# Gate and up pieces of a gated MLP as two lists of equal length

## The chip, the cores and the metric

The kernel runs on one core of a Trainium2 chip. A core has a matrix engine (TensorE, PE in the profile; its weight loads are PEld), VectorE (DVE), ScalarE (ACT), GpSimd (POOL) and SyncE (SP), which issues the DMAs here. Matmul results go to PSUM, which has eight banks of 128 x 512 float32; everything else stands in SBUF. The metric is the device time of one execution in microseconds (us).

## The reference

```python
x = A_x                                     # 1 x 2048 x 576, bf16
xn = _layernorm(x, axis=-1)
qkv = (xn @ wqkv).reshape(B, S, 3, 32, 18)  # 32 heads of 18
...                                         # causal, window of 256, softmax
s = (softmax(q k^T * 18 ** -0.5) @ v).reshape(B, S, 576) @ wo
...
gate = xn @ w_gate                          # 576 x 4608
up = xn @ w_up                              # 576 x 4608
g = silu((sigmoid(gate) * up) @ w_down)     # 4608 x 576
return x + s * g
```

## The kernel before

**Chunks.** The 2048 tokens are worked in four chunks of 512. For each chunk: layer norm, the QKV projection, attention, the output projection (`build_wo`, line 734), gate and up (`build_ffn`, line 777), and the down projection with the final product (`f2`, lines 851 and 881, and `final_cols`). Program order is not execution order: every operation goes into a list with an engine, an estimated duration, a priority and what it depends on, and a planner (`schedule`) places them one after the other in simulated time, lowest estimated start plus priority x 40 ns first. Each engine's order is then fixed, and `emit` writes it out with semaphore waits. SyncE's queue of DMAs is one such order.

**Gate and up.** The hidden width of 4608 is cut into 36 tiles of 128 (`ft`). For one tile, gate and up are each nine matmuls of 64 contraction rows by 512 tokens, since 576 is 9 x 64. The array is used as two halves of 64 rows: gate always in rows 0 to 63, up always in rows 64 to 127, and `xn` and the weights are stored for both halves, in the orders of blocks `LO` and `UP`. A step is one gate piece and one up piece side by side. Gate runs `SKEW` = 3 pieces ahead of up:

```python
def f_a(e, ft=ft):
    for i in range(NA):
        if ft < NFT:
            r = step(e, 0, ft, i)
        if ft > 0:
            r = step(e, 1, ft - 1, NC - NA + i)
    return r
```

so each tile is three TensorE operations of three steps (`fa`, `fb0`, `fb1`). At the start of a chunk's gate/up work three gate pieces have no partner, and at its end three up pieces. Each tile's gate and up take one PSUM bank each, from banks 4 to 7. When gate is complete, ScalarE takes its tanh (line 763); then VectorE forms (tanh + 1) x up into `hT` (line 767), which frees the tile's banks. Weights come in 12 groups of three tiles, four DMAs a group, into a ring of three slots (`wgs`).

**Around it.** Score units of attention (line 589) use banks 0 to 3, all four at once; ScalarE takes their exponentials (line 607), and the value products (line 658) follow for a pair of head groups. The planner puts these units between gate/up operations. In chunk 0, SyncE's queue issues x, the QKV weights, weight groups 0, 1 and 2, then eight transposing DMAs of q and k (line 209), then weight group 3. The output projection's four blocks are copied by ScalarE (line 749) into `sat`, a ring of four slots, one slot a block; `final_cols` reads the slot in the product of line 916.

**The end.** The last output block is done in two column parts, 448 and 128. Each goes through tanh (line 912), two products (914, 916), an addition to x (918) and a store. The load of x for that block is given a slack of 5000 ns in the planner. After its last DMA, SyncE waits for the final value of every DMA semaphore, in order of their numbers, and the program ends:

```python
if e == "SP":
    for ln, v in enumerate(lane_cnt):
        if v > 0:
            eng.wait_ge(lanes[ln], v)
    eng.nop()
```

Of the kernel before, what the change touches and what calls it, by code (L numbers as in the profile page):

```python
# [12 lines left out]
P = 128  # L13
CH = 512
# [6 lines left out]
FG = 3  # L21
# [27 lines left out]
SKEW = 3  # L49
# [6 lines left out]
FB_CUTS = (0,3,6)  # L56
LAST = 448
W_GATE = 2
F2B = ((0, 1), (2, 3), (6, 7), (4, 5))
# [110 lines left out]
class Builder:  # L170
# [97 lines left out]
    def build(self):  # L268
# [22 lines left out]
        for c in range(NCH):  # L291
# [6 lines left out]
            self.build_attn(c)  # L298
            self.op_pkz = [self.op("POOL", 2000, lambda e: e.memset(self.pk[:, 1:RPK, :, :], 0.0), f"pkz:{c}",
# [420 lines left out]
    def build_wo(self, c):  # L720
        self.op_wop = [None] * QPC
        self.op_s = [None] * QPC
        for pair in ((0, 2), (1, 3)):
# [22 lines left out]
            for qi, ps, (ss, _) in zip(pair, ps2, slots):  # L746
# [4 lines left out]
                self.op_s[qi] = (ss, se)  # L751
                self.op_wop[qi] = wo

    def build_ffn(self, c):
        mms = []
        pg, pu, slots, dmas = [], [], [], []
        wrel = {}

        def th_mul(ft, o_g, o_u):
            st_, dt_ = self.r_t.take()  # L760

            def f_th(e, st_=st_, ps=pg[ft]):
                return e.activation(self.tring[:, st_, :], self.bank(ps), ACTF.Tanh, scale=0.5)  # L763
            th = self.rd("ACT", act_ns(CH), f_th, f"th:{c}:{ft}", deps=[o_g] + dt_, prio=1, psum=[pg[ft]])

            def f_mul(e, st_=st_, ft=ft, ps=pu[ft]):
                return e.scalar_tensor_tensor(self.hT[:, ft, :], self.tring[:, st_, :], 1.0, self.bank(ps),  # L767
                                              ALU.add, ALU.mult)
            war = [self.f2_last[ft // WDG]] if self.f2_last else []
            mul = self.rd("DVE", dve_ns(CH), f_mul, f"hm:{c}:{ft}", deps=[th, o_u] + war, prio=1, psum=[pu[ft]])  # L770
# [3 lines left out]
        def step(e, gu, ft, i):  # L774
            r0 = 64 * gu
            fl = ft % FG
            return e.matmul(self.bank((pg, pu)[gu][ft]), self.wgs[r0:r0 + 64, slots[ft // FG], i, fl * P:(fl + 1) * P],  # L777
                            self.xn[r0:r0 + 64, i, :], start=(i == 0), stop=(i == NC - 1), tile_position=(r0, 0))
        NA = SKEW
        for ft in range(NFT + 1):  # L780
            if ft < NFT:
                if ft % FG == 0:
                    fg = ft // FG
                    sw, dw = self.r_w.take()
                    slots.append(sw)
                    wp = W_PRIO[fg] if c == 0 and fg < RW else -2
                    fc = slice(fg * FG * P, (fg + 1) * FG * P)
                    ws = self.load9(self.wgs[0:64, sw, :, :], self.wgs[64:P, sw, :, :], self.wg[:, fc],
                                    self.wu[:, fc], f"w:{c}:{fg}", ("w", sw),
                                    dw + ([self.w_gate] if c > 0 and fg < RW else []), wp,  # L790
                                    W0_FACTOR if c == 0 and fg < 5 else 1.42)
                    dmas.append(ws)
                    if c == 0 and fg in QKT_BEHIND:
                        for o in self.op_qkt[QKT_BEHIND[fg]:]:
                            o.behind = ws[-1:]
                pg.append(Psum((6,), (7,), (5,), (4,)))
                pu.append(Psum((6,), (7,), (5,), (4,)))
            war = [self.f2_last[ft // WDG]] if self.f2_last and ft < NFT else []
# [361 lines left out]
```

## Time and profile before

| | |
|---|---|
| three runs, median (range) | 570.92 us (570.83 to 571.53) |
| the profiled execution | 571.24 us |
| its span, first to last instruction | 569.0 us |
| TensorE busy | 560.6 us (99%) |
| VectorE, ScalarE busy | 304.8 us (54%), 274.7 us (48%) |
| gate and up matmuls, line 777 | 2592, busy 298.8 us |
| down projection matmuls, lines 851 and 881 | 1152, busy 134.4 and 9.0 us |
| exponentials, line 607 | 152, busy 147.2 us |
| DMA moved | 73.03 MB |

Busy time of an engine is the union of its instructions. Matmuls overlap in the records, so the mean of one (377 ns at line 777) is longer than the time from one step to the next. The chain of waits follows the program back from its last instruction, at each step to what released it; its rows give start, length, what ran, and how many instructions in a row. The timeline gives the same instructions by engine, with the idle time before each group and what ended it in brackets. A q behind an engine's name stands for its instruction queue: DMA issues and semaphore checks.

### The profile page before, as it was taken

The numbers are of one execution on the slowest core, as the hardware profiler recorded it, in microseconds if no ns is written. First come the engines' busy times: TensorE is split into PE (matmuls) and PEld (weight loads), VectorE is DVE, ScalarE is ACT, GpSimd is POOL, SyncE is SP. The second block draws the span as 40 slices with busy tenths as digits, with TensorE's granted clock in tenths as the row PEclk, the third lists the DMA queues.
The fourth block names the chain that finished last, engine by engine and source line by source line (L and its number), as shares of the span: only waits on it lengthen the run. The fifth ranks groups of instructions, "written<-read, shape, count | busy, mean of one in ns | idle before, by whom it ended". The sixth has DMA issues, their size and how long they took to land.

```text
span 569.0 us, 17867 instructions
## 1 busy us (share of the span) xinstructions
PE 560.6 (99%) x7854; PEld 284.3 (50%) x7854; DVE 304.8 (54%) x664; ACT 274.7 (48%) x372; POOL 28.2 (5%) x55
## 2 busy tenths in 40 slices
PE   8999999999999999999999999999999999999996
PEld 5634444457544444456654444545754444444543
DVE  6137888732137896661205788765121586675312
ACT  7456666314055856721307576580321856856011
POOL 3000100010000100010000010001000000000100
PEclk9999999999999999999999999999999999999999
DMA  8999998528946765234694665604479455640001
GB/s 198 204 204 250 240 219 204 124 61 117 203 91 145 160 142 136 64 57 92 101 223 95 147 149 125 150 25 73 87 147 176 104 129 122 154 106 23 20 22 43
DMA packets 124874, 73.03 MB, mean 128 GB/s; under 512 B 53630, under 2 KB 124286, under 8 KB 124798
## 3 DMA queue, kind: packets, MB, share of 16 engines
q1 hardware_dynamic: 124798, 71.90, 59.5%
q8 instruction: 62, 1.02, 0.8%
q14 instruction: 14, 0.11, 0.1%
HBM read 55.22 MB, written 2.36 MB: 101 GB/s over the span
## 4 chain that ended last, share of the span: by engine, by line
PE 94%; SPq 2%; DMA 2%; issue 0%; ACT 0%; DVE 0%; DVEq 0%
PE ps L777 50%; PE ps L851 23%; PE ps L460 8%; PE ps L589 5%; PE ps L658 3%; PE ps L734 3%; SPq L210 2%; PE ps L881 2%; DMA wqkv_sb<-in_A_wqkv_dram 1%; DMA wgs<-in_B_w_up_dram 1%; ACT expr L509 0%; DVE xf L918 0%; DVE thf L914 0%; ACT thf L912 0%; DVE thf L916 0%
## 5 line engine op out<-in xcount | busy, mean ns | idle before, releaser
L777 PE MATMUL ps<-xn,wgs 64*128 64x512 bf16 x2592 | 298.8, 377 | 1.2 <-DMA wgs<-in_B_w_up_dram 1.1
L777 PEld LDWEIGHTS ps<-xn,wgs 64*128 64x128 bf16 x2592 | 120.8, 94 | 146.1 <-issue 9.8
L607 ACT ACTIVATE expr<-ps 128x1024 bf16<-128x1024 f32 x152 | 147.2, 1022 | 28.2 <-PE ps L589 28.2
L851 PE MATMUL ps<-wd_sb,hT 128*128 128x512 bf16 (+1 forms) x1080 | 134.4, 286 | 0.0
L763 ACT ACTIVATE tring<-ps 128x512 bf16<-128x512 f32 x144 | 86.3, 599 | 78.6 <-PE ps L777 63.6
L767 DVE SCALAR_TENSOR_TENSOR hT<-tring,ps 128x512 bf16<-128x512 bf16 x144 | 97.5, 677 | 28.5 <-PE ps L777 27.4
L851 PEld LDWEIGHTS ps<-wd_sb,hT 128*128 128x128 bf16 x1080 | 68.0, 98 | 65.7 <-DVE expr L625 1.7
L625 DVE TENSOR_TENSOR expr<-expr,m 128x512 bf16<-128x512 bf16 (+2 forms) x152 | 58.3, 412 | 61.8 <-ACT expr L607 61.0
L912 ACT ACTIVATE thf<-ps 128x576 bf16<-128x576 f32 (+2 forms) x17 | 10.6, 623 | 139.4 <-PE ps L851 132.2
L914 DVE SCALAR_TENSOR_TENSOR thf<-thf,ps 128x576 bf16<-128x576 bf16 (+2 forms) x17 | 12.2, 718 | 104.9 <-ACT thf L912 104.9
L460 PE MATMUL ps<-wqkv_sb,xn 64*128 64x288 bf16 x864 | 54.7, 283 | 0.6 <-DMA wqkv_sb<-in_A_wqkv_dram 0.6
L460 PEld LDWEIGHTS ps<-wqkv_sb,xn 64*128 64x128 bf16 x864 | 42.9, 94 | 11.3 <-issue 1.9
L589 PE MATMUL ps<-qkp 18*64 18x320 bf16 (+4 forms) x1472 | 32.4, 259 | 0.0
L589 PEld LDWEIGHTS ps<-qkp 18*64 18x64 bf16 x1472 | 16.1, 103 | 32.5 <-issue 15.7
L508 DVE CAST pk<-ps 128x576 bf16<-128x576 f32 x15 | 11.3, 755 | 23.0 <-PE ps L460 22.9
L698 DVE STREAM_TRANSPOSE op__63<-pk 128x512 bf16<-128x512 bf16 x32 | 22.3, 696 | 0.3
L636 POOL COPY qkp<-qkp 128x256 bf16<-128x256 bf16 x24 | 9.6, 398 | 248.6 <-PE ps L589 248.6
L676 DVE STREAM_TRANSPOSE pk<-ps 128x512 f32<-128x512 f32 x32 | 21.6, 675 | 0.0
L658 PEld LDWEIGHTS ps<-expr,vau 64*32 64x32 bf16 x1440 | 17.9, 92 | 6.4 <-issue 5.6
L658 PE MATMUL ps<-expr,vau 64*32 64x320 bf16 (+5 forms) x1440 | 20.7, 253 | 0.0
L674 DVE STREAM_TRANSPOSE tf<-ps 128x512 f32<-128x512 f32 x16 | 11.4, 713 | 15.4 <-PE ps L658 15.1
L734 PE MATMUL ps<-wo_sb,oT 64*128 64x512 bf16 (+1 forms) x288 | 18.7, 283 | 0.1
(52 smaller groups left out, 189.1 us busy)
## 6 DMA issues: line engine op xcount, KB each, us to landing
wgs<-in_B_w_gate_dram SPq DMA_DIRECT2D x48, 240.0 KB, 3.9
wgs<-in_B_w_up_dram SPq DMA_DIRECT2D x48, 240.0 KB, 4.7
wgs<-in_B_w_up_dram SPq DMA_DIRECT2D x48, 192.0 KB, 4.1
wgs<-in_B_w_gate_dram SPq DMA_DIRECT2D x48, 192.0 KB, 4.3
wd_sb<-in_B_w_down_dram SPq DMA_DIRECT2D x9, 576.0 KB, 6.3
xf<-in_A_x_dram SPq DMA_DIRECT2D x18, 144.0 KB, 2.2
out_dram<-xf SPq DMA_DIRECT2D x15, 144.0 KB, 1.9
xr<-in_A_x_dram SPq DMA_DIRECT2D x14, 144.0 KB, 4.2
```

The costliest lines, as they stand in the source:

```text
L460: r = e.matmul(self.bank(ps, HV, hf), self.xn[r0:r0 + 64, k, i * P:(i + 1) * P], self.wqkv_sb[r0:r0 + 64, j, k, :], start=(k == 0), stop=( ...
L589: r = e.matmul(self.ps[64 * half:64 * half + 64, b:b + n * 64], self.qkp[r0:r0 + DH, hg, k0:k0 + 64], self.qkp[r0:r0 + DH, hg, q0 * 64:(q0 ...
L607: return e.activation(self.expr[:, es, 2 * pr:2 * pr + 2, :], src, ACTF.Exp, scale=SM_SCALE)
L625: return e.tensor_tensor(ap, ap, m, ALU.mult)
L658: r = e.matmul(self.ps[32 * j:32 * j + 32, b + q0 * 64:b + (q0 + n) * 64], vf[:, v0:v0 + 32], self.expr[p0:p0 + 64, es, j, pos * 64:(pos + ...
L676: t3 = self.rd("DVE", dve_ns(CH), lambda e, tg=tg, hg=hg: e.transpose(tg, self.bank(ps2[hg][1])), f"t3:{c}:{hg}", deps=[o, self.last_mul] ...
L698: t2 = self.op("DVE", dve_ns(CH), lambda e, on=on: e.transpose(self.op_[:, hg % NOT, :], on.rearrange("p g d -> p (g d)")), f"t2:{c}:{hg}" ...
L734: r = e.matmul(self.bank(ps2[w], n1 - n0, n), self.oT[r0:r0 + 64, kt, qi * P:(qi + 1) * P], self.wo_sb[r0:r0 + 64, kt, n0:n1], start=(swap ...
L763: return e.activation(self.tring[:, st_, :], self.bank(ps), ACTF.Tanh, scale=0.5)
L767: return e.scalar_tensor_tensor(self.hT[:, ft, :], self.tring[:, st_, :], 1.0, self.bank(ps), ALU.add, ALU.mult)
L777: return e.matmul(self.bank((pg, pu)[gu][ft]), self.wgs[r0:r0 + 64, slots[ft // FG], i, fl * P:(fl + 1) * P], self.xn[r0:r0 + 64, i, :], s ...
L851: r = e.matmul(self.ps[:, b + n0:b + n1], lhsT, self.wd_sb[:, q, fl, n0:n1], start=(ft == 0), stop=(ft == NFT - 1))
```

## The change

Gate and up pieces are written as two lists, `low` for rows 0 to 63 and `high` for rows 64 to 127, of 324 entries each. Two pieces of one gate tile (tile 10 in chunk 0, tile 1 in the others) go into the upper list, from step 4 of the tile ahead of it, and two pieces of the last up tile into the lower list, just ahead of the last gate tile. Their weights are loaded for the other half by two extra DMAs a chunk (`load_x`) into one slot of `sat`, 64 rows x 256 columns each. That slot also serves the fourth block of the output projection, whose copy now depends on the last gate/up operation.

The lists are cut into TensorE operations wherever a tile changes in either list, and a cut longer than `RUN` = 3 steps once more in the middle. Where a tile passes from one half to the other, the operation waits on TensorE's own semaphore for the last one of the other half (`fence`). Gate has no lead over up ahead of the split tile; behind it gate runs two steps early and up two steps late.

At the end, SyncE's waits for all semaphores but those of the last two stores move ahead of these stores. The last load of x has a slack of 600 ns in the planner in place of 5000.

```diff
@@ -46,16 +46,20 @@
-SKEW = 3
+XS = (10, 1, 1, 1)
+XP = (4, 0)
+RUN = 3
+WX_PRIO = -1
+WX_FT = 7
...
-FB_CUTS = (0,3,6)
 LAST = 448
 W_GATE = 2
+LAST_OUTS = 2
...
             self.build_attn(c)
+            self.load_x(c)
...
         self.op_s = [None] * QPC
+        self.op_se = []
...
                 self.op_s[qi] = (ss, se)
+                if ss == self.sx:
+                    self.op_se.append(se)
                 self.op_wop[qi] = wo
 
+    def load_x(self, c):
+        self.sx, dx = self.r_s.take()
+        f = XS[c] * P
+        src = [(self.wg, f, 1, 64), (self.wu, (NFT - 1) * P, 0, 0)]
+        self.op_wx = []
+        for n, (w, f, j, r0) in enumerate(src):
+            a = w[:, f:f + P].rearrange("(j p) c -> p j c", p=64)[:, j:j + 3:2, :]
+            dst = self.sat[r0:r0 + 64, self.sx, 0:2 * P].rearrange("p (j c) -> p j c", j=2)
+            self.op_wx.append(self.dma(dst, a, 2 * W_FACTOR * 64 * 2 * P * 2, f"wx{n}:{c}", ("wx", n), deps=dx, prio=WX_PRIO))
+            self.r_s.release(self.sx, self.op_wx[-1])
+
     def build_ffn(self, c):
-        mms = []
-        pg, pu, slots, dmas = [], [], [], []
-        wrel = {}
-
-        def th_mul(ft, o_g, o_u):
...
+        xs, xe = XS[c], NFT - 1
+        gp = [i for i in range(NC) if LO[i] not in UP[0:2]]
+        up = [i for i in range(NC) if UP[i] not in LO[0:2]]
+        low, high = [], []
+        for ft in range(NFT):
+            low += [(0, ft, i, None) for i in (gp if ft == xs else range(NC))]
+            high += [(1, ft, i, None) for i in (up if ft == xe else range(NC))]
+        n = NC * (xs - 1) + XP[0]
+        high[n:n] = [(0, xs, 0, 0), (0, xs, 1, 1)]
+        n = len(low) - NC + XP[1]
+        low[n:n] = [(1, xe, 0, 0), (1, xe, 1, 1)]
+        assert len(low) == len(high) == NC * NFT
+        seen, left = set(), {}
+        for k in low + high:
+            left[k[:2]] = left.get(k[:2], 0) + 1
+        cuts = {0, len(low)}
+        for n in range(1, len(low)):
+            if any(st[n][:2] != st[n - 1][:2] for st in (low, high)):
+                cuts.add(n)
+        cuts = sorted(cuts)
+        for n0, n1 in zip(cuts, cuts[1:]):
+            if n1 - n0 > RUN:
+                cuts.append(n0 + (n1 - n0 + 1) // 2)
+        cuts = sorted(cuts)
+        prev = None
...
+        def step(e, half, gu, ft, i, x):
+            r0 = 64 * half
+            f0 = ft % FG * P
+            w = (self.wgs[r0:r0 + 64, slots[ft // FG], i, f0:f0 + P] if x is None
+                 else self.sat[r0:r0 + 64, sx, x * P:(x + 1) * P])
+            first, last = flags[(half, gu, ft, i)]
+            return e.matmul(self.bank((pg, pu)[gu][ft]), w, self.xn[r0:r0 + 64, i, :], start=first, stop=last,
+                            tile_position=(r0, 0))
...
+        def finish(ft):
...
+            th = self.rd("ACT", act_ns(CH), f_th, f"th:{c}:{ft}", deps=[tile_end[(0, ft)]] + dt_, prio=1, psum=[pg[ft]])
...
-            mul = self.rd("DVE", dve_ns(CH), f_mul, f"hm:{c}:{ft}", deps=[th, o_u] + war, prio=1, psum=[pu[ft]])
+            mul = self.rd("DVE", dve_ns(CH), f_mul, f"hm:{c}:{ft}", deps=[th, tile_end[(1, ft)]] + war, prio=1,
+                          psum=[pu[ft]])
...
-        NA = SKEW
-        for ft in range(NFT + 1):
-            if ft < NFT:
...
+        for n0, n1 in zip(cuts, cuts[1:]):
+            deps, alloc, fence, done, ended = [prev], [], None, [], []
+            for n in range(n0, n1):
+                for half, st in enumerate((low, high)):
+                    gu, ft, i, x = st[n]
                     fg = ft // FG
...
-            def f_a(e, ft=ft):
-                for i in range(NA):
-                    if ft < NFT:
-                        r = step(e, 0, ft, i)
-                    if ft > 0:
-                        r = step(e, 1, ft - 1, NC - NA + i)
+                    if x is None and fg not in slots:
+                        sw, dw = self.r_w.take()
+                        slots[fg] = sw
...
+                        if c == 0 and fg == RW:
+                            self.op_wx[1].add_dep(self.op_f1[(0, WX_FT)])
...
+                    key = (gu, ft)
+                    if key not in seen:
+                        seen.add(key)
+                        alloc.append((pg, pu)[gu][ft])
+                        if self.f2_last and gu == 0:
+                            deps.append(self.f2_last[ft // WDG])
+                    if x is None:
+                        deps += dmas[fg]
+                        group_left[fg] -= 1
+                        if group_left[fg] == 0:
+                            ended.append(fg)
+                    else:
+                        deps.append(self.op_wx[gu])
+                    if half != gu or key in ((0, xs), (1, xe)):
+                        if tile_last.get(key, (half,))[0] != half:
+                            fence = tile_last[key][1]
+                    left[key] -= 1
+                    if left[key] == 0:
+                        done.append(key)
+            if not prev:
+                deps += self.all_xn
+
+            def f(e, n0=n0, n1=n1):
+                for n in range(n0, n1):
+                    step(e, 0, *low[n])
+                    r = step(e, 1, *high[n])
-            oa = self.pe(NA * mm_ns(CH), f_a, f"fa:{c}:{ft}",
-                         deps=(dmas[ft // FG] + self.all_xn + war if ft < NFT else []), prio=3,
-                         psum=[pg[ft]] if ft < NFT else [], mode="r64", odeps=mms)
...
-            def f_b(e, ft, i0, i1):
-                for i in range(i0, i1):
-                    step(e, 0, ft, NA + i)
-                    r = step(e, 1, ft, i)
-                return r
-            ob = oa
-            for n, (i0, i1) in enumerate(zip(FB_CUTS, FB_CUTS[1:])):
-                ob = self.pe((i1 - i0) * mm_ns(CH), lambda e, ft=ft, i0=i0, i1=i1: f_b(e, ft, i0, i1), f"fb{n}:{c}:{ft}",
...
-        mms = [oa]
-        self.r_xn.release(0, oa)
+            o = self.pe((n1 - n0) * mm_ns(CH), f, f"f:{c}:{low[n0][1]}:{n0}", deps=deps, prio=3, psum=alloc, mode="r64")
+            if fence:
+                o.add_dep(fence)
+                o.fence = fence
...
+            for key in done:
+                tile_end[key] = o
+                if key[0] == 0:
+                    self.op_f1[(c, key[1])] = o
+                if tile_end.get((1 - key[0], key[1])):
+                    finish(key[1])
+            prev = o
+        for o in self.op_se:
+            o.add_dep(prev)
+        mms = [prev]
+        self.r_xn.release(0, prev)
...
-        sx, o_x = self.load_xf(sb)
+        sx, o_x = self.load_xf(sb, DMA_SLACK_NS)
...
-    def load_xf(self, sb):
+    def load_xf(self, sb, slack=LATE_SLACK):
...
-                            deps=dx + [self.op_hT[NFT - 6]], prio=3, slack=LATE_SLACK)
+                            deps=dx + [self.op_hT[NFT - 6]], prio=3, slack=slack)
...
+            end = [o for o in self.prog[e] if o.lane is not None][-LAST_OUTS:]
             for o in self.prog[e]:
+                if e == "SP" and o is end[0]:
+                    for ln, v in enumerate(lane_cnt):
+                        if v > 0 and not any(self.lane_ids[d.lane] == ln for d in end):
+                            eng.wait_ge(lanes[ln], v)
+                            known[("L", ln)] = v
...
-                    if v > 0:
+                    if v > 0 and known.get(("L", ln), -1) < v:
```

More of the change, by code (lines that the diff above doesn't have):

```diff
@@ new lines, in build_ffn @@
+    def build_ffn(self, c):
+        pg = [Psum((6,), (7,), (5,), (4,)) for _ in range(NFT)]
+        pu = [Psum((6,), (7,), (5,), (4,)) for _ in range(NFT)]
+        slots, dmas = {}, {}
+        xs, xe = XS[c], NFT - 1
[23 more added lines that the diff above has]
+        prev = None
+        tile_end, tile_last = {}, {}
+        def step(e, half, gu, ft, i, x):
[6 more added lines that the diff above has]
+                            tile_position=(r0, 0))
+        sx = self.sx
+        flags, count = {}, {}
+        for n in range(len(low)):
+            for half, st in enumerate((low, high)):
+                gu, ft, i, x = st[n]
+                count[(gu, ft)] = count.get((gu, ft), 0) + 1
+                flags[(half, gu, ft, i)] = (count[(gu, ft)] == 1, count[(gu, ft)] == NC)
+        def finish(ft):
```

65 lines of the change are left out of this document (28 added, 37 removed).

## The prediction

> **What bounds the kernel now.** I read the page first: busy time by engine, the chain that ended last, the costliest groups.
>
> ```profile
> span 569.0 us, 17867 instructions
> ...
> PE 560.6 (99%) x7854; PEld 284.3 (50%) x7854; DVE 304.8 (54%) x664; ACT 274.7 (48%) x372; POOL 28.2 (5%) x55
> ...
> PE   8999999999999999999999999999999999999996
> ...
> PE 94%; SPq 2%; DMA 2%; issue 0%; ACT 0%; DVE 0%; DVEq 0%
> ...
> L777 PE MATMUL ps<-xn,wgs 64*128 64x512 bf16 x2592 | 298.8, 377 | 1.2 <-DMA wgs<-in_B_w_up_dram 1.1
> ```
>
> TensorE is busy for 560.6 of 569.0 us; only the first and the last slice fall short. So time is won in two ways alone: fewer TensorE steps, or a shorter head or tail. Half of the work is L777, the gate and up pieces, and the page shows 1.2 us of idle time before them, nearly all of it one DMA wait. Next I read the chain of waits in order of time, to get the price of one L777 step (columns: start, length, what, how many instructions in a row).
>
> ```profile
> 74.81 4.64 PE ps L777 x42
> ...
> 103.16 2.70 PE ps L777 x21
> ...
> 160.38 2.05 PE ps L777 x15
> ...
> 377.56 2.70 PE ps L777 x24
> 380.61 2.70 PE ps L777 x21
> 383.32 1.09 PE ps L851 x8
> ...
> 437.98 2.05 PE ps L777 x15
> 440.03 0.35 PE ps L589 x16
> 440.38 2.70 PE ps L777 x24
> ```
>
> A step is one piece in row half 0 to 63 beside one in rows 64 to 127. From 24 to 42 matmuls, nine steps more, the stretch grows by 1.94 us: 0.216 us a step. The last stretch of a chunk's gate/up work holds 21 matmuls, three fewer than 24, and also takes 2.70 us. So its last three up pieces, which have no partner, cost a full step each. The first stretch of 15 takes 2.05 us, 0.65 or three steps less than 24: nine steps, three of them gate pieces alone.
>
> **The change part by part.**
>
> *Equal lists.* Before, gate runs three pieces ahead of up: 36 x 9 + 3 = 327 steps a chunk. After, each half has a list of exactly 324, because two gate pieces went to the upper list and two up pieces to the lower. Four chunks: 4 x 3 x 0.216 = 2.59 us off TensorE. All of it lies on the path, since nothing but TensorE is on it there. The number of matmuls does not change.
>
> [...]
>
> *Order within the lists.* In chunks 1 to 3 the two gate pieces enter the upper list at step 4 and those of the last up tile enter the lower list nine steps before its end. Between these points gate runs two steps early and up two late, so gate leads by four steps where it led by three. Tanh then starts a step earlier relative to the product; bank reuse (four banks, two a tile) gets no tighter: nine steps, 1.94 us, from a tile's end to its bank's next use, as before. In chunk 0 tiles 0 to 9 have no lead: tanh and product then follow each other after the tile. Their rows in the stretch without attention work:
>
> ```profile
> 29.05 0.60 ACT L763 ACTIVATE tring<-ps 128x512 bf16<-128x512 f32 x1 [1.34 <-PE ps L777]
> 29.76 0.69 DVE L767 SCALAR_TENSOR_TENSOR hT<-tring,ps 128x512 bf16<-128x512 bf16 x1 [1.26 <-PE ps L777]
> ```
>
> From tanh's start to the product's end is 1.40 us; with 0.16 before it (a matmul lasts 377 ns, a step 216) that makes 1.6 of 1.94. It fits, with 0.3 to spare, for as long as ScalarE is free. I take nothing; if it failed, 0.3 us a tile for eight tiles is 2.4.
>
> *Fences.* The first piece of the split gate tile in the lower half waits until its upper pieces have landed in the bank, and the split up tile the other way: two waits a chunk on TensorE's own semaphore. Behind each stand all later TensorE instructions, and ScalarE's tanh waits for those. The work waited for was issued three steps earlier at the gate tile and two at the up tile; a matmul lasts 377 ns, under two steps. The nearest row is the fence of the attention projection, which directly follows the work that it waits for:
>
> ```profile
> 541.24 1.35 PE ps L734 x20
> 542.59 0.05 issue
> 542.64 2.38 PE ps L734 x36
> ```
>
> Bounds: 0 to 8 x 0.05 = 0.4 us; I take 0.1.
>
> *Eight extra loads of 32 KB.* In chunks 1 to 3 they go out after the previous chunk's first output block has read its slot of the projection buffer, long before the next gate/up stage begins. In chunk 0 the gate pieces' load has the priority -1, between the last QKV weights and weight group 1, so it is issued ahead of groups 1 and 2 and of the transposes. That queue is late already:
>
> ```profile
> 19.40 9.04 SPq L209 DMA_TRANSPOSE qkp<-pk  x3
> ...
> 28.48 7.14 SPq L209 DMA_TRANSPOSE qkp<-expr  x5
> ...
> 35.67 0.62 SPq L210 DMA_DIRECT2D wgs<-in_B_w_gate_dram  x1
> ...
> 41.62 0.43 SPq L210 DMA_DIRECT2D wd_sb<-in_B_w_down_dram  x1
> ...
> 42.65 0.82 PE L777 MATMUL ps<-xn,wgs 64*128 64x512 bf16 x6 [1.06 <-DMA wgs<-in_B_w_up_dram]
> ```
>
> Weight group 3 is issued from 35.67 on, behind eight transposes, and TensorE waits 1.06 us for it at step 81. Step 81 needs the same 81 steps after the change, so nothing won before it counts. One more issue of 0.43 us ahead in the queue makes that wait longer by at most that. From below: the group's ring slot is released at step 27 in place of 30, which could bring it ahead of the last transposes and take the whole 1.06 away. Bounds -1.06 to +0.43; I take +0.3, as the queue's order is most likely the same.
>
> *The held projection.* The fourth output block's copy (line 749) now waits for the end of the gate/up stage, since its slot holds the extra weights. What stands behind it on ScalarE are output tanhs. The projection runs well after that stage (chunk 3: stage ends at 522, projection at 541.24, above), so the wait has been met; nothing. If it ran inside the stage, two of TensorE's banks would be held until the end.
>
> *Smaller pieces of work.* Gate/up operations were three steps; now they are 3, 2, 2, 2 of every nine (5 and 4 in chunk 0 before tile 10). Score units can only enter between them. They entered every 12 steps:
>
> ```profile
> 443.01 0.43 PE L589 MATMUL ps<-qkp 18*64 18x320 bf16 x24
> 443.37 2.76 PE L777 MATMUL ps<-xn,wgs 64*128 64x512 bf16 x24
> 446.06 0.42 PE L589 MATMUL ps<-qkp 18*64 18x256 bf16 x16
> ```
> ```profile
> 443.56 1.94 ACT L607 ACTIVATE expr<-ps 128x1024 bf16<-128x1024 f32 x2 [0.49 <-PE ps L589]
> 445.38 0.60 ACT L763 ACTIVATE tring<-ps 128x512 bf16<-128x512 f32 x1
> ```
> ```profile
> 438.00:522.00 84.00, 84.00 (x1320) 37.87 (x1320) 56.18 (x115) 58.49 (x77) 0.00 (x0) 1.00 0.47 110
> ```
>
> The period is 3.05 us. The unit's banks come free when its exponentials end, 445.50, 2.5 us after its start. The new cuts allow 11 steps, 2.83 us, still above 2.5, but ScalarE would then do 1.94 of exponentials and 1.2 tanhs of 0.60 in it: 2.7 of 2.83. Over the whole stage ScalarE has 58.5 of 84 us to do and the same after (last row, the stage of chunk 3). Bounds: 0, and the rival below; I take 0.2.
>
> *Closing waits.* The end, from timeline, issue list and the line of the waits:
>
> ```profile
> 558.96 0.34 SPq L210 DMA_DIRECT2D xf<-in_A_x_dram  x1
> ...
> 563.22 0.39 DVE L916 TENSOR_TENSOR thf<-thf,sat 128x448 bf16<-128x448 bf16 x1
> ...
> 564.62 0.22 DVE L916 TENSOR_TENSOR thf<-thf,sat 128x128 bf16<-128x128 bf16 x1
> 564.77 0.52 DVE L918 TENSOR_TENSOR xf<-xf,thf 128x448 bf16<-128x448 bf16 x2
> 565.18 0.81 SPq L210 DMA_DIRECT2D out_dram<-xf  x2
> ```
> ```profile
> L1095 SPq EVENT_SEMAPHORE  x41: 17/28/28, 566.0 to 568.5; - x41
> ```
> ```profile
> out_dram<-xf SPq DMA_DIRECT2D x1, 32.0 KB, 1.6
> ```
>
> Before, SyncE issues both last stores and then checks 41 instructions' worth of semaphores one after another, 566.0 to 568.5; then 0.5 us of closing to 569.0. The last store starts at about 565.6 and lands 1.6 later, at 567.2: it is the checks that end the program. After, all but the two last stores' checks stand ahead of those stores, between the load at 558.96 and the first store. They need 2.5 us and have from 559.3 to 564.0; what stands behind them is only the two stores.
>
> The shorter slack of the last load makes the planner put the wide addition (L918, 448 columns) right after its product at 563.61, where it stood behind the narrow product. Then the narrow addition, 0.22 us, ends at about 565.06 and its store starts at 565.2 in place of 565.6. End: 565.2 + 1.6 + 0.5 = 567.3, 1.7 us earlier. Bounds: 1.3 without the reordering, 1.8.
>
> **The sum.** -2.59 - 1.7 + 0.1 + 0.3 + 0.2 = -3.7 us. The profiled execution took 571.24 (span 569.0 and 2.24 around it): 567.5. It lies 0.32 above the median of 570.92, so I forecast 567.2.
>
> **The rivals.**
>
> *ScalarE becomes the bound* (slower). In the 60 score units of chunks 1 to 3 a tanh of 0.60 gets between a unit's exponentials and the next unit, which waits on TensorE, in order, for the banks. A unit that holds a tanh frees its banks after 2.5 + 0.6 = 3.1 us, 0.3 past a period of 2.83. It decides from 3.7 / 60 = 62 ns a unit on; with 0.3 in half of the units the loss is 9 us: 576. For it speaks the 2.7 of 2.83; against it that exponentials and tanhs are only 70% of the stage, and that the trace has no such wait before L589.
>
> *Chunk 0 gives back* (less gain): eight tiles without a lead lose 0.3 each, or the first weights come later: +2.1, 569.3. Against it: the wait at step 81 covers part of what is lost before it.
>
> *Group 3 gets ahead of the transposes*: -1.06 in place of +0.3, 565.8.
>
> *The unpaired pieces cost nothing*, as the halves find partners across operations, so that the lists save nothing: 569.8. The 21-matmul rows speak against it.
>
> [...]
>
> **How the numbers follow.** Forecast 0.66; ScalarE 0.09; chunk 0 gives back 0.12; group 3 early 0.08; no saving from lists 0.03; open weight loads 0.02. The range, 565.4 to 569.8, leaves out ScalarE and spares 0.4 us below the lowest case. Less than 0.2% (1.14 us) can't be told from no change, so faster means under 569.8: forecast, early group, weight loads and most of "gives back", 0.85; same 0.06; slower 0.09.
>
> **What would show it.** Right: the gate/up stretches between two score units hold as many matmuls in each half, and no stretch of 21 costs as much as 24; the closing checks stand before 564; the last store starts near 565.2 minus 2 to 3 us; DMA wait at step 81 of about 1.4 us; no idle time before L589. Wrong: idle time on TensorE before L589 or L777 put down to ScalarE or VectorE in chunks 1 to 3, or a wait of several us in chunk 0.

## The result, and the profile after

The changed kernel takes 568.14 us (median of six runs, 567.31 to 569.12) where the kernel before took 570.88 us (six runs, 570.52 to 571.53): a ratio of 0.9949, 95% interval 0.9939 to 0.9959. The forecast was 567.2 us in a range of 565.4 to 569.8. The profiled execution took 567.65 us, with a span of 565.0 against 569.0. One of the changed kernel's runs in the experiments, 575.61 us at a mean clock of 0.991, counts as slow and is left out of its ratio.

From the page of the changed kernel:

```profile
span 565.0 us, 17870 instructions
...
PE 555.0 (98%) x7830; PEld 283.0 (50%) x7854; DVE 307.4 (54%) x664; ACT 274.6 (49%) x372; POOL 28.2 (5%) x55
...
PE   8999999999999999999999999999999999999997
...
PE 94%; SPq 2%; DMA 1%; issue 1%; DVE 1%; ACT 0%
...
L810 PE MATMUL ps<-xn,wgs 64*128 64x512 bf16 x2576 | 296.3, 377 | 1.4 <-ACT expr L612 1.4
```

TensorE is still what sets the end. (24 of its 7854 matmuls, all of the down projection L930, are missing from this trace, so its busy time reads slightly low.) L810 is the old L777; it now has one wait of 1.4 us ahead of it instead of one of 1.1.

The chain of waits in chunk 1 (start, length, what, how many in a row):

```profile
160.28 2.05 PE ps L810 x18
162.68 2.48 PE ps L810 x22
165.52 2.70 PE ps L810 x24
...
240.83 2.92 PE ps L810 x26
```

The first stretch now does 18 matmuls in the 2.05 us in which 15 were done. The last does 26 in 2.92, one step of 0.22 more than 24 in 2.70, where 21 had taken as long as 24: no piece pays for an empty half any more. Score units enter after 22 or 24 matmuls. The gate/up stage of chunk 1 as a whole, before and then after, from the table of stretches (stretch and its length, then busy time and count of PE, PEld, DVE, ACT, POOL, then granted clock, DMA share, GB/s):

```profile
160.28:244.31 84.03, 84.03 (x1322) 37.91 (x1320) 60.99 (x135) 58.40 (x77) 5.38 (x12) 1.00 0.51 117
```
```profile
160.20:243.58 83.38, 83.38 (x1322) 37.65 (x1320) 60.53 (x134) 57.92 (x76) 5.38 (x12) 1.00 0.52 118
```

As many matmuls, no idle time in either, and 0.65 us less: three steps of 0.216. The waits of TensorE from chunk 1 to the end show what did not happen:

```profile
PE ps L930 <- issue: 0.6, 4, 0.2
PE ps L930 <- ACT sat L755: 0.2, 1, 0.2
PE ps L930 <- DVE hT L828: 0.2, 1, 0.2
PE ps L930 <- DVE tf L684: 0.2, 1, 0.2
```

Nothing before L810 or L594 (the scores): no ScalarE bound, no fence that stops anything. The seven gaps before L930 are 0.16 us each and stand where matmuls are missing from the trace; a later profile of the same kernel, with all 7854, shows no wait at all from chunk 1 to the end. Chunk 0 differs. TensorE's timeline there, and the queue of DMA issues:

```profile
40.39 1.04 PE L810 MATMUL ps<-xn,wgs 64*128 64x512 bf16 x8
42.79 1.04 PE L810 MATMUL ps<-xn,wgs 64*128 64x512 bf16 x8 [1.37 <-ACT expr L612]
```
```profile
27.85 7.86 SPq L213 DMA_TRANSPOSE qkp<-expr  x5
...
35.76 0.60 SPq L214 DMA_DIRECT2D wgs<-in_B_w_gate_dram  x1
...
37.73 0.62 SPq L214 DMA_DIRECT2D wgs<-in_B_w_up_dram  x1
```

The wait at step 81 grew from 1.06 to 1.37 us. The engine named, ScalarE, had ended at 42.53; the group's fourth load was issued at 37.73 and took 4.7 us, so it landed at 42.44 and is what the step waits for, as before the change, when it landed at 42.40. In all five profiles with the lists the step starts 0.35 us after this landing, whatever ScalarE does; in the four without them that the table on chunk 0 shows, 0.25 us after it. So of the 0.31 by which the wait grew, 0.16 is TensorE reaching the step earlier (41.43 for 41.59), 0.10 the longer way from landing to start, and 0.04 a later landing.

The end, from the timeline, the lines of the two sets of checks, and the issue list:

```profile
556.94 0.34 SPq L214 DMA_DIRECT2D xf<-in_A_x_dram  x1
...
561.62 0.39 DVE L997 TENSOR_TENSOR xf<-xf,thf 128x448 bf16<-128x448 bf16 x1
562.10 1.34 SPq L214 DMA_DIRECT2D out_dram<-xf  x2
562.60 0.22 DVE L995 TENSOR_TENSOR thf<-thf,sat 128x128 bf16<-128x128 bf16 x1
562.86 0.23 DVE L997 TENSOR_TENSOR xf<-xf,thf 128x128 bf16<-128x128 bf16 x1
```
```profile
L1159 SPq EVENT_SEMAPHORE  x41: 28/28/28, 557.3 to 560.2; - x41
```
```profile
L1181 SPq EVENT_SEMAPHORE  x1: 17/17/17, 564.6 to 564.6; - x1
```
```profile
out_dram<-xf SPq DMA_DIRECT2D x1, 32.0 KB, 1.5
```

The 41 checks now run from 557.3 to 560.2, 1.9 us before the first store is due. The wide addition follows its product, the second store goes out at 563.1 when the narrow addition is done, and one last check at 564.6 is followed by the end at 565.0.

**Where the 4.0 us of span went.** Starts of the QKV projections and of the last output block's matmuls, from both traces:

| | before | after | gained in the stretch |
|---|---|---|---|
| QKV of chunk 0 | 7.21 | 7.20 | 0.01 |
| QKV of chunk 1 | 124.69 | 124.59 | 0.09 |
| QKV of chunk 2 | 263.57 | 262.86 | 0.61 |
| QKV of chunk 3 | 402.39 | 401.04 | 0.64 |
| last output block | 554.96 | 552.94 | 0.67 |
| end | 569.0 | 565.0 | 1.94 |

Three chunks give their three steps each, the tail gives 1.94, and chunk 0 gives almost nothing. The experiments ask about the two parts of the change apart, the price of a step and of a fence, and chunk 0.

### The profile page after: what moved, and what is told of

Read it like the earlier page. It is cut to its first block, busy times and chain, and to the rows that moved or that the text cites. A ratio compares the mean times of both kernels' runs of the same rounds, so it can differ in the third digit from the quotient of the medians.

```text
span 565.0 us, 17870 instructions
## 1 busy us (share of the span) xinstructions
PE 555.0 (98%) x7830; PEld 283.0 (50%) x7854; DVE 307.4 (54%) x664; ACT 274.6 (49%) x372; POOL 28.2 (5%) x55
## 4 chain that ended last, share of the span: by engine, by line
PE 94%; SPq 2%; DMA 1%; issue 1%; DVE 1%; ACT 0%
PE ps L810 50%; PE ps L930 23%; PE ps L465 8%; PE ps L594 5%; PE ps L663 4%; PE ps L740 3%; SPq L214 2%; PE ps L960 2%; DMA wqkv_sb<-in_A_wqkv_dram 1%; ACT sat L755 0%; ACT expr L612 0%; DVE tf L679 0%; DVE hT L828 0%; DVE pk L681 0%; DVE tf L684 0%
## 5 line engine op out<-in xcount | busy, mean ns | idle before, releaser
L810 PE MATMUL ps<-xn,wgs 64*128 64x512 bf16 x2576 | 296.3, 377 | 1.4 <-ACT expr L612 1.4
L810 PEld LDWEIGHTS ps<-xn,wgs 64*128 64x128 bf16 x2576 | 119.4, 94 | 143.7 <-issue 8.9
L930 PE MATMUL ps<-wd_sb,hT 128*128 128x64 bf16 (+1 forms) x1056 | 131.0, 284 | 2.2 <-issue 1.0
L930 PEld LDWEIGHTS ps<-wd_sb,hT 128*128 128x128 bf16 x1080 | 68.1, 98 | 65.0 <-issue 1.4
L594 PEld LDWEIGHTS ps<-qkp 18*64 18x64 bf16 x1472 | 16.2, 103 | 32.6 <-ACT expr L612 14.0
L594 PE MATMUL ps<-qkp 18*64 18x320 bf16 (+4 forms) x1472 | 32.4, 259 | 0.1
```

The costliest lines, as they stand in the source:

```text
L594: r = e.matmul(self.ps[64 * half:64 * half + 64, b:b + n * 64], self.qkp[r0:r0 + DH, hg, k0:k0 + 64], self.qkp[r0:r0 + DH, hg, q0 * 64:(q0 ...
L810: return e.matmul(self.bank((pg, pu)[gu][ft]), w, self.xn[r0:r0 + 64, i, :], start=first, stop=last, tile_position=(r0, 0))
L930: r = e.matmul(self.ps[:, b + n0:b + n1], lhsT, self.wd_sb[:, q, fl, n0:n1], start=(ft == 0), stop=(ft == NFT - 1))
```

## The experiments

Each ratio below is against the kernel before in runs on the same chip, with its 95% interval. One per cent is 5.7 us.

**The three parts apart.** First the changed kernel with the old end:

```diff
-        sx, o_x = self.load_xf(sb, DMA_SLACK_NS)
+        sx, o_x = self.load_xf(sb)
...
-                if e == "SP" and o is end[0]:
+                if e == "SP" and o is None:
```

> The change's two lists alone: the closing waits stay behind the last stores and the last load of x keeps its slack of 5000 ns. My theory: the time is gained in two places that add up, so this kernel is 2.0 us faster than before (0.6 us a chunk from the unpaired steps in chunks 1 to 3, 0.1 in chunk 0), and its last 14.0 us, from the start of the last block's matmuls to the end, are as before. Rival: on the chip where the changed kernel was 1.2 us slower, the lists bring less than 1 us, and the lost time is in chunk 0, ahead of step 85.

Measured: 570.05 us, ratio 0.9975 (0.9959 to 0.9990), so -1.4 us (-2.3 to -0.6). In its profile the stages of chunks 1 and 2 last 83.38 us, as in the changed kernel, and the tail 14.10, as before it. Chunk 0 took longer, and shows how. The timeline at step 81, and the stretch behind it:

```profile
43.63 1.04 PE L810 MATMUL ps<-xn,wgs 64*128 64x512 bf16 x8 [1.72 <-ACT tring L824]
```
```profile
44.00:45.00 1.00, 1.00 (x34) 0.47 (x30) 0.58 (x2) 0.00 (x0) 0.00 (x0) 0.96 1.15 205
45.00:48.00 3.00, 3.00 (x24) 1.07 (x18) 0.76 (x2) 2.54 (x3) 0.00 (x0) 0.50 1.14 226
```

A wait of 1.72 us, and 1.3 us after it the granted clock falls to 0.50 for 3.41 us (44.92 to 48.34). At half the clock that is an estimated 1.7 us more; from step 81 to the QKV projection of chunk 1 this profile took 83.04 us, where two of the changed kernel without such a stretch took 81.39 and 81.40. So chunk 0 paid here for the wait and about as much again behind it.

Then the kernel before with the closing checks moved, and nothing else:

```diff
+            end = [o for o in self.prog[e] if o.lane is not None][-2:]
             for o in self.prog[e]:
+                if e == "SP" and o is end[0]:
+                    for ln, v in enumerate(lane_cnt):
+                        if v > 0 and not any(self.lane_ids[d.lane] == ln for d in end):
+                            eng.wait_ge(lanes[ln], v)
+                            known[("L", ln)] = v
...
-                    if v > 0:
+                    if v > 0 and known.get(("L", ln), -1) < v:
```

> The kernel before with the closing waits ahead of the last two stores, and nothing else. My theory: the end is then set by the last store's landing, 1.6 us after its issue at 565.6, so the program ends 1.3 us earlier. Rival: the checks run beside the landing and cost nothing, 0 us; or moved ahead they delay the first of the two stores, and less than 0.8 us is left.

Measured: 570.02 us, ratio 0.9981 (0.9968 to 0.9995), -1.1 us; in the profile the tail fell from 14.05 to 12.71, 1.34 less. Its checks and its last stores:

```profile
L1080 SPq EVENT_SEMAPHORE  x40: 27/28/28, 559.1 to 561.9; - x40
```
```profile
564.52 0.52 DVE L918 TENSOR_TENSOR xf<-xf,thf 128x448 bf16<-128x448 bf16 x2
564.99 0.81 SPq L210 DMA_DIRECT2D out_dram<-xf  x2
```

The checks are out of the way by 562; both additions still run together at 564.5. Then the kernel before with the shorter slack alone:

```diff
-        sx, o_x = self.load_xf(sb)
+        sx, o_x = self.load_xf(sb, DMA_SLACK_NS)
...
-    def load_xf(self, sb):
+    def load_xf(self, sb, slack=LATE_SLACK):
...
-                            deps=dx + [self.op_hT[NFT - 6]], prio=3, slack=LATE_SLACK)
+                            deps=dx + [self.op_hT[NFT - 6]], prio=3, slack=slack)
```

> The kernel before with the last load of x planned with a slack of 600 ns in place of 5000, and nothing else. My theory: the wide addition moves ahead of the narrow product, the last store is issued 0.4 us earlier, the checks behind it start 0.4 us earlier, and the program is 0.4 us faster. Rival: no change, since the end is set by the checks and not by the store: 0 us.

Measured: 570.38 us, ratio 0.9991 (0.9977 to 1.0005), not to be told from no change by time; but the profile's tail is 13.53, 0.52 less, and shows the mechanism:

```profile
562.67 0.39 DVE L918 TENSOR_TENSOR xf<-xf,thf 128x448 bf16<-128x448 bf16 x1
563.09 1.41 SPq L210 DMA_DIRECT2D out_dram<-xf  x2
563.65 0.23 DVE L916 TENSOR_TENSOR thf<-thf,sat 128x128 bf16<-128x128 bf16 x1
563.91 0.23 DVE L918 TENSOR_TENSOR xf<-xf,thf 128x128 bf16<-128x128 bf16 x1
```

The wide addition goes ahead of the narrow product, and its store no longer holds up the narrow one. The whole change beside these three:

> The changed kernel again, on the same chip as the parts. My theory: the parts add up, the lists' gain plus 1.7 for waits and slack together, 567.2 against 570.9. Rival: 568.7 as in the slower three of its runs, with the 1.2 us between them in the wait for weight group 3 in chunk 0.

Measured: 568.70 us, ratio 0.9948 (0.9928 to 0.9969), -3.0 us: the sum of the three parts, -1.4 - 1.1 - 0.5. Nothing here says that the parts hinder each other; as each difference is known to some 0.8 us only, this does not show that they add up exactly.

**The price of an unpaired step.** The kernel before with the lead doubled, so that six pieces a chunk stand alone at each end:

```diff
-SKEW = 3
+SKEW = 6
...
-FB_CUTS = (0,3,6)
+FB_CUTS = (0,3)
```

> The kernel before with gate six pieces ahead of up in place of three, so six steps without a partner at each end of a chunk's gate/up work and 330 steps in place of 327. My theory: an unpaired step costs a full 0.216 us, so 12 more steps make the kernel 2.6 us slower. Rival: unpaired pieces find partners across operations and cost nothing, 0 us. [...]

Measured: 578.89 us, ratio 1.0138 (1.0120 to 1.0156), +7.9 us. From one QKV projection to the next, chunks 1 and 2 grew by 0.78 and 0.74 us, and chunk 3 up to the last block by 0.71: 0.24 to 0.26 a step, for three more steps. In the profile chunk 0 grew by 4.63 us, its own three steps among them, with two waits and a stretch at half clock, and the end came out 0.52 us shorter, as with the shorter slack. The timeline in chunk 0:

```profile
42.66 1.47 PE L777 MATMUL ps<-xn,wgs 64*128 64x512 bf16 x12 [1.48 <-ACT expr L607]
...
99.87 1.80 PE L777 MATMUL ps<-xn,wgs 64*128 64x512 bf16 x12 [2.33 <-DMA wgs<-in_B_w_up_dram]
```
```profile
101.00:104.00 3.00, 3.00 (x38) 1.16 (x36) 1.77 (x3) 1.65 (x2) 0.00 (x0) 0.50 0.76 217
```

So a step costs what a matmul's step costs (the coarser cut of the work is in these numbers too). And chunk 0 answers a shift of a few steps with several us.

**The price of a fence.** The changed kernel with the extra pieces placed so that each fence stands directly behind the work that it waits for:

```diff
-XP = (4, 0)
+XP = (7, 2)
```

> The changed kernel with the pieces of the split tiles moved right ahead of the other half's first piece (steps 7 and 8 in place of 4 and 5 of the tile ahead; two steps later in the lower list), so that each of the eight fences stands directly behind the work that it waits for. My theory: in the changed kernel a fence costs at most 0.1 us in all; directly behind, each costs the rest of a matmul and the semaphore's way, 0.2 to 0.4 us, 2 to 3 us in all. Rival: a fence costs nothing wherever it stands, 0 us, or it costs the same 0.05 us as the one in the output projection.

Measured: 577.67 us, ratio 1.0116 (1.0103 to 1.0129): against the changed kernel's 0.9949 some 9.5 us slower. The timeline of chunk 1's split tile:

```profile
168.54 0.37 PE L810 MATMUL ps<-xn,wgs 64*128 64x512 bf16 x1 [0.60 <-DVE thf L993]
...
168.77 0.38 PE L810 MATMUL ps<-xn,sat 64*128 64x512 bf16 x1
169.20 1.25 PE L810 MATMUL ps<-xn,wgs 64*128 64x512 bf16 x10
```

The pieces read from `sat` are the moved ones. The step behind them starts at 169.20, 0.43 us after the last instead of 0.216: the fence costs 0.22 us, one whole step. That is the same in chunks 1 to 3, at both tiles (0.223 three times at the gate tile; 0.23 at the up tile), so the six fences of these chunks cost 1.35 us. Of the 0.22, only 0.05 is idle time in the record: the other 0.16 is the overlap of one matmul (377 ns) with the next step (216 ns), which the fence takes away. The greater part of the loss is elsewhere: gate/up steps that start 0.28 to 0.60 us late in every chunk, such as the one behind the wait of 0.60 in the first row, which are put down to VectorE and ScalarE and whose cause stays open; and chunk 0, whose gate/up stage took 93.26 us in place of 87.77, with 3.41 us at a granted clock of 0.50 in it. The planned order is another one too: in chunk 1 the first value products start 8 us into the gate/up stage (174.04) in place of 17. So the 9.5 us are not the price of the fences; the 0.22 is. In the changed kernel, with two and three steps between, neither the 0.22 nor these waits are seen in chunks 1 to 3.

**The wait at step 81.** Both kernels wait there for weight group 3, which is issued behind eight transposes. If that order is the cause, issuing the group ahead of the last two transposes should free more than a microsecond. In the changed kernel, and then in the kernel before:

```diff
-QKT_BEHIND = {2: 0}
+QKT_BEHIND = {2: 0, 3: 6}
```

> The changed kernel with weight group 3 of chunk 0 issued ahead of the last two of the eight transposes instead of behind them. My theory: the wait at step 81 of chunk 0 (1.4 to 1.7 us in the changed kernel, sometimes followed by 3.4 us at half TensorE clock, 1.7 us more) is the difference between the slow and the fast runs of the changed kernel. Without it the kernel is 1.4 to 3 us faster than the changed one, 566 or below, and its runs lie closer together. Rival: the first score unit starts 2.6 us later and the lost time comes back where chunk 0's attention ends: no gain.

> The kernel before with the same move of weight group 3. My theory: it loses its wait of 0.6 to 1.1 us at step 81 and is 0.8 us faster than before; and the distance to the changed kernel with the same move, where chunk 0's wait plays no part in either, is the full worth of the change, 2.6 us for the lists and 1.9 for the end, 4.5 us. Rival: the lists are worth only 2.0 in this pair too, so that chunk 0's loss has another cause than this wait.

Measured: 571.01 us, ratio 0.9991 (0.9968 to 1.0014), with runs from 566.45 to 574.37; and for the kernel before 571.55 us, ratio 1.0009 (1.0000 to 1.0018). The wait at 81 went away in both. In the first, TensorE's waits in chunk 0 became

```profile
PE ps L810 <- DMA wgs<-in_B_w_up_dram: 4.7, 3, 2.8
```

three waits for weights of 4.7 us together, the longest at 99.8 to 102.6, followed by a stretch at a granted clock of 0.50 (103.94 to 107.36). In the second, one wait took its place:

```profile
59.55 2.76 PE L777 MATMUL ps<-xn,wgs 64*128 64x512 bf16 x24 [0.93 <-issue]
```

and the gate/up stage of chunk 0 lasted 87.91 us as before. So the order decides where TensorE waits, but putting it right gained nothing in the median. The table of stretches of the changed kernel suggests why the wait only moves (20 to 42 and 46 to 80 lie in chunk 0, the last in chunk 1; the two last numbers are DMA share and GB/s):

```profile
20.00:42.00 22.00, 21.34 (x256) 11.01 (x252) 6.21 (x10) 10.67 (x16) 0.40 (x1) 1.00 1.11 197
46.00:80.00 34.00, 33.85 (x544) 15.40 (x540) 28.46 (x69) 20.45 (x29) 2.82 (x6) 1.00 1.11 237
160.00:243.00 83.00, 83.00 (x1320) 37.52 (x1318) 59.95 (x133) 57.54 (x76) 5.38 (x12) 1.00 0.52 119
```

In these stretches of chunk 0 the DMA share is 1.11, so the engines have none left; in the gate/up stage of chunk 1 it is 0.52, and half is free. That what is moved forward in that queue moves something else back fits this, and is not shown by itself. (Two of the twelve runs of the first kernel, 566.45 and 566.95, had a mean clock of 1.000 and are as fast as the fastest of the changed kernel; the mean of its clock fell to 0.994 in the slowest. The profiled run took 573.50.)

**The early load.** Then the other suspect: chunk 0's 32 KB load ahead of weight groups 1 and 2. The changed kernel with that load issued behind weight group 3, the changed kernel again, and the kernel before with the early load alone:

```diff
+                            self.op_wx[0].add_dep(self.op_f1[(0, 2)])
```

> The changed kernel with chunk 0's early extra load (32 KB of gate weights, issued ahead of weight group 1) moved behind weight group 3 in SyncE's queue; all other orders are the same. My theory: this load, ahead of two weight groups and eight transposes in a queue that is already late, delays weight group 3; without it the wait at step 81 falls from 1.4 to 1.7 us back to the 0.6 to 1.1 us of before, and the kernel is 0.6 us faster than the changed one in the same job. Rival: chunk 0 moves as fast as its DMAs can, and the wait stays as long or comes back as another wait for weights later in chunk 0: within 0.3 us of the changed kernel.

> The changed kernel, beside the one with the late load on the same chip. Both theories: 567.3 to 568.8 against 570.9, with chunk 0 no shorter than before, chunks 1 and 2 shorter by 0.65 us each, and 12.1 us from the start of the last block's matmuls to the end.

```diff
+            if c == 0:
+                f = 10 * P
+                src = self.wg[:, f:f + P].rearrange("(j p) c -> p j c", p=64)[:, 1:4:2, :]
+                dst = self.sat[64:P, 0, 0:2 * P].rearrange("p (j c) -> p j c", j=2)
+                self.op_wx0 = self.dma(dst, src, 2 * W_FACTOR * 64 * 2 * P * 2, "wx0", ("wx", 0), prio=-1)
...
```

(In the line left out here, the projection's copies of chunk 0 wait for this load, since one of them writes to its slot.)

> The kernel before with the early 32 KB load alone, at the same place in SyncE's queue; nothing reads what it loads. My theory: weight group 3 lands later, the wait at step 81 grows by 0.5 us or more, and the kernel is 0.5 us slower than before. Rival: the load is too small to matter, 0 us, and the longer wait of the changed kernel comes from the order of its gate and up pieces.

Measured: 568.42 us, ratio 0.9944 (0.9927 to 0.9961), with the load late; 568.08 us, 0.9941 (0.9925 to 0.9958), for the changed kernel; 571.52 us, 1.0003 (0.9993 to 1.0012), for the early load alone. The load costs nothing that can be measured, early or late; by the interval of the last kernel it costs at most 0.7 us. Their waits at step 81, in this order, with one for a transpose ahead of it in the first:

```profile
37.30 0.42 PE L594 MATMUL ps<-qkp 18*64 18x320 bf16 x16 [0.67 <-DMA qkp<-expr]
...
43.24 1.04 PE L810 MATMUL ps<-xn,wgs 64*128 64x512 bf16 x8 [1.06 <-DMA wgs<-in_B_w_up_dram]
```
```profile
42.95 1.04 PE L810 MATMUL ps<-xn,wgs 64*128 64x512 bf16 x8 [1.20 <-ACT expr L612]
```
```profile
41.96 0.82 PE L783 MATMUL ps<-xn,wgs 64*128 64x512 bf16 x6 [0.95 <-DMA wgs<-in_B_w_up_dram]
```

**Chunk 0 in the profiles.** Cut at step 81, its two parts tell different things. The table has the profiles with weight group 3 in its old place and the lists, leads and fences of one of the two kernels. Times from the first QKV matmul of chunk 0 to step 81, and from there to the QKV projection of chunk 1:

| kernel | lists | early load | to step 81 | step 81 to QKV of chunk 1 | in the second part |
|---|---|---|---|---|---|
| before | no | no | 35.44 | 82.04 | |
| before, checks moved | no | no | 34.60 | 82.17 | |
| before, slack | no | no | 34.51 | 82.04 | |
| before, early load | no | yes | 34.73 | 82.88 | a wait of 0.62 at the value products |
| after | yes | yes | 35.59 | 81.80 | value products 0.41 longer |
| after, second profile | yes | yes | 36.31 | 81.40 | |
| after, third profile | yes | yes | 35.80 | 81.39 | |
| after, late load | yes | no | 35.87 | 82.85 | a wait of 1.21 at the value products |
| after, old end | yes | yes | 35.76 | 83.04 | half clock, 1.7 |

The second part takes 82.04 without the lists and 81.39 with them where nothing disturbs it: 0.65, the three steps, are saved here too. The first part comes out longer with the lists in each of the profiles, on average 35.87 against 34.82, though its number of steps is the same. These are nine profiles, one each, and the group's loads land with differences of this size from run to run; but the two sets do not overlap, and two profiles that are not in the table fall on the same sides (35.45 for the doubled lead, 36.16 for the fences directly behind their work). Of the 1.05 us between the averages, 0.10 is the longer way from landing to start; the rest is the landing. The row for the early load alone, at 34.73, and the one with the lists and a late load, at 35.87, speak for the lists and against the load. They do not show it: in the late-load profile one issue of group 3 took 1.35 us in place of 0.62, and without those 0.7 us its row could lie among the kernels without lists. Why group 3 lands later with the lists is not settled: the amount loaded up to there differs by 32 KB at most, and the queue's order is otherwise the same. No kernel with lists and another order of chunk 0's tiles was tried. The longer value products and the waits ahead of them are not a mark of the lists either, since the early load alone has one.

## Why the prediction came out as it did

The forecast was 567.2, the median 568.14: right in sign, and in the range, with 0.9 us less gain. The three pairings of the changed kernel with the one before give 2.9, 3.0 and 3.4 us by their ratios (0.9949, 0.9948, 0.9941), so the shortfall from 3.7 is some 0.3 to 0.8 us. Step by step:

- *Equal lists, -2.59.* The mechanism and the price hold. Three steps are 0.65 us in the stages of chunks 1 and 2 (84.03 to 83.38), and 0.65 in chunk 0 behind step 81. No run shows the open weight loads to which the forecast gave 0.02: with a load of 94 ns, the mean at line 777 before, on top of 0.216, a step would come to 0.31 and a stage to 0.93 less, and the stages came out 0.65 shorter. As the doubled lead gave 0.24 to 0.26, with a coarser cut in it, I keep 0.216.
- *Order within the lists, nothing.* Right in chunks 1 to 3, where TensorE waits for no bank. Right in chunk 0 too, as far as the rows say: the tiles without a lead show no wait of 0.3 each, only the one at step 81.
- *Fences, +0.1.* They cost 0 in chunks 1 to 3. Directly behind their work they cost 0.22 each; it is the distance of two and three steps that hides them, as the prediction argued. Its upper bound of 0.05 each, from the projection's fence, was four times too low for the uncovered case, since that row shows idle time alone and not the overlap that is lost.
- *Eight extra loads, +0.3.* **This is the term that was mis-sized.** In the profiled run the wait at step 81 did grow by the 0.3 foreseen (1.06 to 1.37), but that it fits is luck: the landing moved by 0.04 only, and with the load late the step comes no earlier, with the load alone no later. The prediction took the arrival of group 3 as fixed by one queue's order, to within one issue of 0.43 us. It varies by more than that from run to run: step 81 starts 34.51 to 35.44 us after the first QKV matmul in four profiles without the lists, and with the lists it came 1.05 us later on average. By these profiles the term is about 1 us and not 0.3. That is in part the second case of the "chunk 0 gives back" rival, the first weights coming later, and not its first, eight tiles without a lead. Why they come later stays open.
- *Smaller pieces and ScalarE, +0.2.* It cost nothing. Score units did come every 11 steps (2.48 us of L810 for 22 matmuls, for 2.70), or 12, and no wait stands before L594 in chunks 1 to 3. The rival in which ScalarE becomes the bound did not happen.
- *The end, -1.7.* It gave 1.94: 1.34 from the checks alone (1.3 was the bound without reordering), 0.52 from the addition moved ahead (0.4 foreseen). The last store was to start 2 to 3 us before 565.2; it starts at 563.1 and lands in 1.5 us instead of 1.6.
- *Group 3 ahead of the transposes, -1.06, as a rival.* It did not come about. When it was made to, the wait went and the gain did not come: the other wait is paid later. So that rival's price was wrong as well: it took the whole wait as gain, and counted on no other wait behind it.

Part of the closeness is luck. The allowances for fences and ScalarE, 0.3 together, were not needed and the end gave 0.24 more than forecast; they make up for most of what chunk 0 cost beyond its 0.3. With 1.05 at step 81 the terms come to -2.59 - 1.94 + 1.05 = -3.5 us, which is more than two of the three pairings gave; the later waits of chunk 0 and the half clock behind some of them could be the rest, and no run separates them.

In the profiled run the terms add up: 4 x 0.65 - 0.15 - 0.41 + 1.94 = 4.0 us, the whole gain of its span, where 0.15 is how much later step 81 came after the first QKV matmul, and 0.41 the length added to the value products at 73.63. The six runs of the changed kernel were 567.31 to 567.65 and 568.64 to 569.12; the profile is one of the first kind, which may be why it fits the forecast (567.5 for the profiled execution, 567.65 measured) better than the median does. A later set of six, 567.32 to 569.47, fills the gap between the two. That the upper ones are due to waits in chunk 0 and the clock behind them fits the spread of chunk 0 in the table, but none of those three runs was itself profiled.

No kernel tried here had a faster median than the changed one.

## What to carry to other kernels

Price a saving by the stage in which it lies: a step on a saturated TensorE was worth its full 0.216 us here wherever no wait for weights stood behind it. In chunk 0, where the DMA engines are full (a share of 1.11), TensorE reached such a wait 0.16 us earlier and gained nothing by it, and a wait that was taken out at one place came back at another. A synchronisation between two halves of the array was free with two or three steps between it and the work that it waits for, and cost a whole step, 0.22 us, with none. The closing checks of a program's DMA semaphores are work like any other: put ahead of the last stores, in time that was idle anyway, they cost nothing that shows, and the tail was 1.34 us shorter.

## What the runs showed of the hardware

- **Half clock after a short wait.** A wait of 1.72 us in TensorE (with the lists and the old end), of 1.86 (fences directly behind their work), of 2.33 (doubled lead) and of 2.82 (group 3 early) each came with 3.41 us at a granted clock of 0.50, which began between 0.1 us before the end of the wait and 1.3 us after it; waits of up to 1.62 us in other places did not.
- **Start records and semaphores tell the order of the two row halves differently.** In the start of chunk 3's gate/up stage before the change, three gate pieces are issued without partners, ahead of the first pair. In the records the matmuls start in pairs from the first, 13 to 19 ns apart (437.914 and 437.927, ..., 439.004 and 439.023), and three come last, alone, at 439.22, 439.44 and 439.65. But the semaphore of the operation whose last matmul is recorded at 439.023, and so ends by 439.40, was raised at 440.05, as late as if the pieces ran in the program's order, and the tanh that waits for it starts at 440.07. So the start records alone do not show that the halves run on their own; both readings give the nine steps of that stretch.
- **A chain of checks.** 41 instructions that check semaphores already met take 2.5 us on SyncE's queue before the change, 566.0 to 568.5, with 28 ns recorded for each: about 61 ns apart. After it they run from 557.3 to 560.2, and 0.4 us of these 2.9 is one check that waits for the last load of x, which landed at 559.07.
